# Ten more operands of layer 2 turned in squares, and the last stage's order made anew

## The chip, the core and the metric

The kernel runs on one core of a Trainium2 chip. Its time is the device time of one execution in microseconds (us). Five engines work at once, each through its own row of instructions, in order: TensorE (PE), VectorE (DVE), ScalarE (ACT), GpSimd (POOL) and SyncE (SP), which issues the DMAs. A semaphore makes one wait for another.

## What is computed

Two blocks stand in a layer, and there are two layers; the reference calls the layers' blocks A and B, twice over 2048 tokens of width 576, in single precision:

```python
x = A_x
x = x + _A_ref(_layernorm(x), A_wqkv, A_wo)                        # layer 1
x = x + _B_ref(_layernorm(x), B_w_q, B_k1, B_k2, B_u, B_v)
x = x + _A_ref(_layernorm(x), A_wqkv, A_wo)                        # layer 2
x = x + _B_ref(_layernorm(x), B_w_q, B_k1, B_k2, B_u, B_v)
```

A is linear attention with 32 heads of 18: q, k, v = x @ wqkv; phi(t) = (t + 1 if t > 0 else exp(t)) + 1e-6; kv = the sum over tokens of phi(k) v, z = the sum of phi(k); o = phi(q) kv / (phi(q) z + 1e-6); then o @ wo. B is a mixture of 64 experts, each one row of u and of v: for each of 32 heads the best of 8 first keys and of 8 second keys is picked (K = 1), and the output is the sum over the heads of gelu(x . u[e]) v[e]. The softmax over one pick is 1.

## The kernel before, in words

The 2048 tokens are 16 tiles of 128; the code numbers the layers 0 and 1, and a name such as `ppo1_7` is of layer 1 and tile 7. TensorE's products keep single precision by splitting each operand into two parts, hi and lo, and adding hi x hi, hi x lo and lo x hi (`product`, L258). An operand must have its channels on the partitions, so a tile of tokens is turned first. There are two ways:

- `transposed` (L215): TensorE turns five blocks of 128x128 into PSUM; ScalarE makes hi (L117), VectorE makes lo = source - hi (L118).
- `squares` over `moved`: VectorE turns the 20 squares of 32x32 of each 128x640 tile in place (L229, the tiles `rf`, `ro`, `rb`), SP stores the result (L231, `y_d`) and reads it back in four loads (L237) that put the squares where they belong, and the same two splits follow. The table `SQUARES` at the head of the kernel says which (layer, tile) take this way, for the operands f (input of k, v, q), o (input of the product with wo) and b (input of block B). `turned` chooses by it.

A tile's steps in block A of layer 2 are the late q (`lq`: product with the q weights, then phi on ScalarE, L284 to L286, and one sum on VectorE, L287), `num` (back_scale: GpSimd multiplies by z, L453, VectorE sums it, L456, inverts and multiplies, L460 and L461), `oT` (turning o), `O` (the product with wo, `ppo`, L483, then the residual x, L473, and the layer norm). In block B they are `bT` (turning y), `S` (scores, `pps`, L525), `sel` (VectorE picks the experts in 14 instructions, L553 to L590, whose last writes `cg`), `gel` (the gelu on ScalarE and GpSimd), the turning of `cg` by TensorE (in one transpose), and `po` (the product with v, L609, and the residual x, L473). In the kernel before, the token `bc1.2,0` turns the b of tile 2 and the cg of tile 0 in one group of six TensorE transposes and one pair of splits; `bT` and `cT` are the two apart, cT with one transpose (L512).

The order of the work is written out by hand: `play` runs the steps of a text in the order of its tokens (`x2` runs two pieces of a step at once), and `in_order` pins the order of PE, ACT, DVE and POOL to it. So no engine takes an instruction ahead of the one that stands before it. SP follows the order of the program. The last text holds the end of layer 0 and all of layer 1, from about 423 us on.

Of the kernel before, what the change touches and what calls it, by code (L numbers as in the profile page):

```python
# [64 lines left out]
def network(ctx, tc, x_in, wqkv, wo, wq_t, k_t, u_t, v2, c_mask, c_mask4, c_ident, c_code, c_code1, c_scale, c_shift, out):  # L65
# [809 lines left out]
    with in_order(*ALL):  # L875

        play("""
            bT0.13 gel0.12 po0.11 sel0.12 v1.10 po0.11x2 gel0.12 num0.15 sel0.12 k1.10 bT0.13 v1.10 sel0.12 fT1.11
            sel0.12 oT0.14 v1.10 fT1.11 O0.14 num0.15 cT0.12 num0.15 k1.10 cT0.12 O0.14 oT0.15 bT0.13 po0.12 S0.13
            O0.14 fT1.11 S0.13 oT0.15 po0.12x3 sel0.13x2 v1.11 gel0.13 fT1.12 gel0.13 oT0.15 O0.14 sel0.13x2 k1.11  # L880
            v1.11 O0.15 fT1.12 O0.15 bT0.14 st1.10 cT0.13 v1.11 bT0.14 S0.14 cT0.13 O0.15 fT1.12 keep1.12 po0.13 k1.11
            S0.14 gel0.14 sel0.14 po0.13 gel0.14 st1.11 po0.13 k1.12 sel0.14x2 po0.13 fT1.13 k1.12 O0.15 v1.12x2
            sel0.14 v1.12 bT0.15 cT0.14x2 st1.12 fT1.13 bT0.15 po0.14 S0.15 po0.14 fT1.13 S0.15 po0.14 ldx1.1 po0.14
            ldx1.3 v1.13 fT1.14 v1.13 sel0.15x3 gel0.15 k1.13 fT1.14 gel0.15 bT0.-1 v1.13 sel0.15 cT0.15 v1.14 cT0.15
            po0.15 k1.13 q1.13 bT0.-1 po0.15 q1.13 v1.14 po0.15x2 v1.14 k1.14 wl1.0 st1.13 fT1.15x2 k1.14 k1.15 v1.15
            rl1.0 st1.14 k1.15 ldq1.13 v1.15x2 rl1.2 st1.15 lq1.0 mk1.0 zs1.0 M1.1 rl1.1 lq1.0 M1.1 rl1.3 ldx1.0 zs1.0
            M1.4x2 M1.3 lq1.1 M1.0 num1.13 num1.0 num1.13 num1.0x2 M1.3 keep1.11 lq1.1 num1.1 M1.0 oT1.0x2 num1.1
            M1.2x2 rl1.4 num1.1 num1.13 lq1.2 O1.0 oT1.1 oT1.13 q1.14 lq1.2 O1.0 oT1.1 O1.0x2 num1.2 q1.14 lq1.3x2
            num1.2 oT1.13 bc1.0,-9 num1.3 O1.1 bc1.0,-9 num1.2 S1.0 O1.1 oT1.2 S1.0 num1.3 lq1.4 gel1.0 num1.3 oT1.2
            O1.1x2 O1.2 bc1.1,-9 sel1.0 gel1.0 ldx1.2 sel1.0 lq1.4 O1.13 rl1.6 bc1.1,-9 sel1.0 num1.4x2 S1.1 O1.2x2  # L890
            ldx1.13 O1.13 S1.1 lq1.6 O1.2 sel1.0 sel1.1 bc1.2,0 rl1.5 ldx1.5 rl1.7 num1.4 oT1.3 ldq1.14 lq1.5 lq1.6
            gel1.1 bc1.2,0 oT1.4 gel1.1 sel1.1 O1.13 rl1.8 sel1.1 S1.2 po1.0 oT1.3 lq1.5 sel1.1 S1.2 O1.3 po1.0 sel1.2
            rl1.9 O1.13 oT1.4 num1.6 bc1.13,1 num1.5 sel1.2 num1.5 lq1.7 bc1.13,1 gel1.2x2 num1.5 S1.13 O1.3 lq1.7
            O1.3x2 num1.6 rl1.11 sel1.2 po1.1 oT1.5 q1.15 oT1.5 ldx1.4 sel1.2 bc1.3,2 po1.1 S1.13 gel1.13 num1.6 O1.4
            bc1.3,2 sel1.13 q1.15 ldx1.6 po1.2 O1.5 oT1.6 ldq1.15 po1.2 sel1.13 num1.14 S1.3 O1.4 lq1.8 O1.4 num1.14
            num1.7 rl1.10 sel1.13 gel1.13 O1.5 num1.14 O1.4 num1.7 S1.3 sel1.13 ldx1.7 sel1.3 oT1.6 num1.7 bc1.4,13
            ldx1.14 bc1.4,13 rl1.12 O1.6 ldx1.8 lq1.8 po1.13 O1.5 gel1.3 O1.5 sel1.3 oT1.7 po1.13 sel1.3 num1.8 O1.6
# [59 lines left out]
```

## Time and profile before

| | us |
|---|---|
| median of three runs (lowest, highest) | 719.56 (718.05, 720.6) |
| the profiled execution | 718.14 |
| its span | 716.4 |
| TensorE busy in it | 699.6 |
| VectorE busy | 475.1 |
| ScalarE busy | 321.6 |
| GpSimd busy | 201.6 |

The span is the time from the first to the last instruction of the profile; 1.74 us lie around it. Busy time is the time in which an engine runs at least one instruction. In a row of the timeline, "x5" is a group of equal instructions run one after another, its length reaches from the first start to the last end, and "[0.48 <-DVE cg L590]" is idle time before it and what ended it. Tiles are named without their numbers in the profile, so `ptb<-ident,yb` is any tile's turning of b.

### The profile page before, as it was taken

How to read it: one execution, taken by the hardware profiler on the slowest of the kernel's cores; microseconds unless marked ns; L12 is line 12 of the kernel's file. 1: busy time of each engine (PE TensorE's matmuls, PEld its weight loads, DVE VectorE, ACT ScalarE, POOL GpSimd, SP SyncE). 2: the span in 40 equal slices, each digit the busy share in tenths (PEclk: the TensorE clock that was granted, in tenths of full speed). 3: DMA queues.
4: the chain of work that ended last, by engine and by line, in shares of the span. 5: the costliest groups of instructions: out<-in, count | busy, mean ns of one | idle time of the engine just before them, and what ended most of it. 6: DMA issues, size and time to landing. Idle time of an engine off the chain costs nothing.

```text
span 716.4 us, 14695 instructions
## 1 busy us (share of the span) xinstructions
PE 699.6 (98%) x5464; PEld 650.7 (91%) x5464; DVE 475.1 (66%) x1031; ACT 321.6 (45%) x658; POOL 201.6 (28%) x543
## 2 busy tenths in 40 slices
...
GB/s 270 291 164 243 266 234 262 247 192 175 108 1 64 103 101 91 162 216 215 245 218 233 212 196 175 168 44 128 149 120 84 97 86 125 47 67 34 67 17 66
DMA packets 82711, 107.17 MB, mean 150 GB/s; under 512 B 8976, under 2 KB 47376, under 8 KB 82640
## 3 DMA queue, kind: packets, MB, share of 16 engines
...
q14 instruction: 28, 0.23, 0.1%
...
## 4 chain that ended last, share of the span: by engine, by line
PE 82%; DVE 8%; ACT 4%; issue 2%; DMA 2%; POOL 1%; SPq 0%; DVEq 0%; ACTq 0%; POOLq 0%
PE ppk L258 15%; PE ppv L258 14%; PE ppq L258 14%; PE ppo L483 12%; PE pps L525 7%; PE kva L525 5%; PE kva L360 3%; PE fold_ps L641 2%; PE po L609 2%; PE ptb L215 2%; PE m L414 1%; PE pto L215 1%; DVE x L473 1%; PE ppq L270 1%; PE ppk L270 1%
## 5 line engine op out<-in xcount | busy, mean ns | idle before, releaser
L483 PE MATMUL ppo<-ohi,thio 126*128 126x252 f32 (+1 forms) x320 | 50.5, 300 | 2.6 <-ACT thio L117 2.6
L483 PEld LDWEIGHTS ppo<-ohi,thio 126*128 126x128 f32 (+1 forms) x320 | 44.8, 189 | 4.4 <-ACT thio L117 3.1
L258 PE MATMUL ppk<-whi,thif 128*128 128x252 f32 (+1 forms) x300 | 45.3, 298 | 0.8 <-ACT thif L117 0.8
L188 ACT ACTIVATE junk<-x,mb 128x576 bf16<-128x576 f32 x32 | 24.8, 775 | 45.2 <-POOL mb L187 44.9
L453 POOL TENSOR_TENSOR o<-pq,zb 128x576 f32<-128x576 f32 x19 | 27.4, 1441 | 62.2 <-ACT zb L399 58.6
L258 PE MATMUL ppv<-whi,thif 128*128 128x252 f32 (+1 forms) x300 | 44.7, 295 | 0.1
L258 PEld LDWEIGHTS ppk<-whi,thif 128*128 128x128 f32 x300 | 40.9, 188 | 4.0 <-issue 2.9
L205 ACT ACTIVATE yb<-x,rsb 128x640 f32<-128x640 f32 x32 | 29.5, 921 | 33.3 <-POOL rsb L195 33.3
L179 POOL TENSOR_SCALAR rsf<-mvf 128x1 f32<-128x1 f32 x16 | 3.4, 212 | 145.3 <-DVE mvf L176 145.2
L258 PE MATMUL ppv<-whi,tlof 128*128 128x252 f32 (+1 forms) x300 | 43.9, 293 | 0.0
L258 PE MATMUL ppk<-whi,tlof 128*128 128x252 f32 (+1 forms) x300 | 43.9, 293 | 0.0
L258 PEld LDWEIGHTS ppv<-whi,thif 128*128 128x128 f32 x300 | 41.3, 188 | 1.0 <-issue 0.4
L258 PEld LDWEIGHTS ppk<-whi,tlof 128*128 128x128 f32 x300 | 41.2, 188 | 0.0
L258 PEld LDWEIGHTS ppv<-whi,tlof 128*128 128x128 f32 x300 | 41.2, 188 | 0.0
L483 PE MATMUL ppo<-olo,thio 126*128 126x252 f32 (+1 forms) x256 | 39.6, 293 | 0.0
L258 PE MATMUL ppq<-whi 128*128 128x252 f32 (+1 forms) x260 | 39.5, 299 | 0.0
L483 PE MATMUL ppo<-ohi,tloo 126*128 126x252 f32 (+1 forms) x256 | 39.4, 293 | 0.0
L277 DVE TENSOR_SCALAR ek<-ek 128x576 f32<-128x576 f32 x16 | 7.3, 457 | 46.4 <-ACT ek L276 46.4
L258 PEld LDWEIGHTS ppq<-whi 128*128 128x128 f32 x260 | 36.0, 188 | 0.6 <-DVE eq L287 0.3
L483 PEld LDWEIGHTS ppo<-olo,thio 126*128 126x128 f32 x256 | 36.2, 188 | 0.0
L483 PEld LDWEIGHTS ppo<-ohi,tloo 126*128 126x128 f32 x256 | 36.1, 188 | 0.0
L258 PE MATMUL ppk<-wlo,thif 128*128 128x252 f32 x240 | 36.1, 293 | 0.0
(205 smaller groups left out, 1784.6 us busy)
## 6 DMA issues: line engine op xcount, KB each, us to landing
...
```

Source lines behind the costliest of these rows:

```text
L188: nc.scalar.activation(junk, xt, AF.Square, bias=m[:, 0:1], accum_out=m[:, 1:2])
L205: nc.scalar.activation(y, x2, AF.Identity, scale=rs[:, 0:1], bias=rs[:, 1:2])
L215: nc.tensor.transpose(pt[:, b * P:(b + 1) * P], x, ident)
L258: nc.tensor.matmul(o[:, at:at + c1 - c0], tt[a == "lo"][:, b, :], wb[:, cols + c0:cols + c1], start=(i == 0), stop=(i == len(todo) - 1))
L270: nc.tensor.matmul(p[:, at:at + c1 - c0], tt[a == "lo"][:, b, :], wb[:, cols + c0:cols + c1], start=(i == 0), stop=(i == len(todo) - 1))
L277: nc.vector.tensor_scalar(e, e, 1.0, EPS, op0=ALU.min, op1=ALU.add)
L360: nc.tensor.matmul(a[64 * h:64 * h + 64, c * 72:c * 72 + n], vt[:, 2 * c + h], fk[:, f0:f0 + n], start=(t == 0 and c == 0), stop=(t == NT ...
L453: nc.gpsimd.tensor_tensor(o[:, :D], pq, zb, op=ALU.mult)
L483: nc.tensor.matmul(p[:, at:at + c1 - c0], hl[a][:r, b], w[:r, c0:c1], start=(i == 0), stop=(i == len(todo) - 1))
L525: nc.tensor.matmul(p[:, :512], hl[a == "lo"][:, b, :], shi[:, b] if w == "hi" else slo[:, blocks(REM)[b][1]], start=(i == 0), stop=(i == l ...
L609: nc.tensor.matmul(p[:, at:at + c1 - c0], c[i], vmix[:, c0:c1], start=(i == 0 and not based), stop=(i == 1))
L641: nc.tensor.matmul(p[32 * j:32 * j + 32, at:at + c1 - c0], kpad[:, ch // 2, 24 - 8 * a:56 - 8 * a], st[:, c0:c1], start=(a == 0), stop=(a ...
```

## The change

Ten operands of layer 1 leave TensorE's way for the squares: o of tiles 3 to 6, and b of tiles 2 to 6 and 13. The six b stood in a group with a cg (bc), which is now turned alone. So TensorE loses 50 transposes, VectorE gains 10 transposes in squares and 6 small splits, ScalarE 6 small splits, and SP 10 stores and 40 loads.

```diff
 SQUARES = {
     "f": {(0, t) for t in range(4, NT)} | {(1, t) for t in range(3, 14)},
-    "o": {(0, t) for t in range(6, NT)},
-    "b": {(0, t) for t in range(5, 14)},
+    "o": {(0, t) for t in range(6, NT)} | {(1, t) for t in range(3, 7)},
+    "b": {(0, t) for t in range(5, 14)} | {(1, t) for t in range(2, 7)} | {(1, 13)},
 }
...
-            O1.1x2 O1.2 bc1.1,-9 sel1.0 gel1.0 ldx1.2 sel1.0 lq1.4 O1.13 rl1.6 bc1.1,-9 sel1.0 num1.4x2 S1.1 O1.2x2
+            cT1.0 oT1.3 oT1.4 lq1.6 sel1.1 po1.0 rl1.9 po1.0 gel1.1 oT1.4 lq1.5 lq1.6 gel1.1 bT1.2 O1.13 sel1.1 num1.5
...
```

The text of the last stage is new as a whole (40 lines); what it moves is seen on the engines. Names end in the number of a tile and a running number.

ScalarE around the split of the b of tile 2 (`thib1_2`) in layer 1, before; `eq1_5` and `eq1_6` belong to the phi of tiles 5 and 6:

```order
L284 ACTIVATE eq1_6_7428<-ppq1_6_7323 128x576
L285 ACTIVATE ppq1_6_7323<-ppq1_6_7323 128x576
L286 ACTIVATE eq1_6_7428<-eq1_6_7428 128x576
L539 ACTIVATE g1_1_7433<-s1_1_7309 128x64
L117 ACTIVATE thib1_2_7377<-ptb1_2_7370 128x768
L543 ACTIVATE g1_1_7433<-g1_1_7433 128x64
L188 ACTIVATE junk_85,mb1_13_7457<-x11_13_7319,mb1_13_7457 128x576
L117 ACTIVATE thio1_3_7395<-pto1_3_7389 128x640
L284 ACTIVATE eq1_5_7493<-ppq1_5_7399 128x576
L285 ACTIVATE ppq1_5_7399<-ppq1_5_7399 128x576
L286 ACTIVATE eq1_5_7493<-eq1_5_7493 128x576
L530 ACTIVATE s1_2_7483<-pps1_2_7468 128x512
```

And now:

```order
L286 ACTIVATE eq1_5_7486<-eq1_5_7486 128x576
L284 ACTIVATE eq1_6_7491<-ppq1_6_7429 128x576
L285 ACTIVATE ppq1_6_7429<-ppq1_6_7429 128x576
L286 ACTIVATE eq1_6_7491<-eq1_6_7491 128x576
L543 ACTIVATE g1_1_7475<-g1_1_7475 128x64
L117 ACTIVATE thib1_2_7347<-gb1_2_7342 128x640
L205 ACTIVATE yb1_13_7505<-x11_13_7335,rsb1_13_7501 128x640
L530 ACTIVATE s1_2_7531<-pps1_2_7516 128x512
```

The split of tile 2 stood after the phi of tile 6 and ahead of that of tile 5; now it comes behind the phi of tile 6 and the tanh of tile 1 (`g1_1`), and reads a loaded tile (`gb1_2`) in place of PSUM (`ptb1_2`).

TensorE at the same place, before: the end of a q product, then scores of tile 2 (`pps1_2`):

```order
L258 MATMUL ppq1_5_7399<-whi_76 128x324
L215 MATMUL pto1_4_7439<-ident_66,o1_4_7289 128x128 x5
L525 MATMUL pps1_2_7468<-shi_80,thib1_2_7377 128x512 x5
L525 MATMUL pps1_2_7468<-slo_81,thib1_2_7377 128x512 x4
L525 MATMUL pps1_2_7468<-shi_80,tlob1_2_7378 128x512 x5
L609 MATMUL po1_0_7485<-vmix_82,thib1_2_7377 128x252
L609 MATMUL po1_0_7485<-vmix_82,thib1_2_7377 128x324
L609 MATMUL po1_0_7485<-vmix_82,tlob1_2_7378 128x252
```

And now:

```order
L258 MATMUL ppq1_6_7429<-whi_76 128x324
L609 MATMUL po1_0_7464<-vmix_82,chi1_0_7404 128x252
L609 MATMUL po1_0_7464<-vmix_82,chi1_0_7404 128x324
L609 MATMUL po1_0_7464<-vmix_82,clo1_0_7405 128x252
L609 MATMUL po1_0_7464<-vmix_82,clo1_0_7405 128x324
L525 MATMUL pps1_2_7516<-shi_80,thib1_2_7347 128x512 x5
L525 MATMUL pps1_2_7516<-slo_81,thib1_2_7347 128x512 x4
L525 MATMUL pps1_2_7516<-shi_80,tlob1_2_7348 128x512 x5
L483 MATMUL ppo1_3_7534<-ohi_78,thio1_3_7411 128x252
```

The five transposes of o of tile 4 are gone from the row, `po1_0` has moved ahead of the scores, and the q product in front of them is that of tile 6 in place of tile 5.

VectorE near the split of the b of tile 4 (`tlob1_4`), before:

```order
L118 TENSOR_TENSOR tloo1_6_7825<-pto1_6_7818,thio1_6_7824 128x640
L460 RECIPROCAL r1_7_7943<-den1_7_7922 128x32
L461 TENSOR_TENSOR o1_7_7896<-eq1_7_7640,r1_7_7943 128x576
L118 TENSOR_TENSOR tlob1_4_7955<-ptb1_4_7947,thib1_4_7954 128x768
L287 SCALAR_TENSOR_TENSOR eq1_8_7993<-eq1_8_7993,ppq1_8_7861 128x576
L565 SCALAR_TENSOR_TENSOR m41_3_8016<-m1_3_7938 128x256
L567 SCALAR_TENSOR_TENSOR m21_3_8018<-m41_3_8016 128x128
L569 SCALAR_TENSOR_TENSOR cd1_3_8020<-m21_3_8018 128x32
L571 SCALAR_TENSOR_TENSOR m21_3_8018<-m21_3_8018 128x32
L473 SCALAR_TENSOR_TENSOR x21_13_8031,sumx21_13_8032<-po1_13_7998,x11_13_7319 128x576
L574 TENSOR_TENSOR oh1_3_8035<-cd1_3_8020,code_w_70 128x256
L577 TENSOR_TENSOR pr1_3_8037<-oh1_3_8035,m21_3_8018 128x512
```

And now:

```order
L571 SCALAR_TENSOR_TENSOR m21_3_8017<-m21_3_8017 128x32
L118 TENSOR_TENSOR tlob1_4_7972<-gb1_4_7966,thib1_4_7971 128x640
L229 STREAM_TRANSPOSE rb1_5_8032<-yb1_5_8030 128x5x4x32
L473 SCALAR_TENSOR_TENSOR x21_13_8043,sumx21_13_8044<-po1_13_8010,x11_13_7335 128x576
L287 SCALAR_TENSOR_TENSOR eq1_8_8047<-eq1_8_8047,ppq1_8_7906 128x576
L574 TENSOR_TENSOR oh1_3_8056<-cd1_3_8019,code_w_70 128x256
L577 TENSOR_TENSOR pr1_3_8058<-oh1_3_8056,m21_3_8017 128x512
L581 TENSOR_REDUCE pi1_3_8060<-pr1_3_8058 128x16
L473 SCALAR_TENSOR_TENSOR x11_6_8093,sumx11_6_8094<-ppo1_6_8064,x1_6_7896 128x576
L584 TENSOR_TENSOR ct1_3_8114<-pi1_3_8060,shift_71 128x64
```

A transpose in squares (`rb1_5`, the b of tile 5) now stands behind the split of tile 4, the select steps of tile 3 (`cd1_3`, `oh1_3`, `pr1_3`) are around it, and the residual of tile 13 (`x21_13`) comes ahead of the phi sum of tile 8.

TensorE in the layer before, near the scores of tile 14 (`kva1`, written with `thib0_14`; other rows of `kva1` are the state of layer 1), before:

```order
L483 MATMUL ppo0_15_6073<-olo_79,tloo0_15_5954 128x324
L215 MATMUL ptb0_14_6112<-ident_66,yb0_14_6029 128x128 x5
L360 MATMUL kva1_3751<-ek1_10_5905,v5_0_86 64x72 x8
L360 MATMUL kva1_3751<-ek1_10_5905,v5_0_86 64x36 x2
L512 MATMUL ptc0_13_6130<-ident_66,cg0_13_6040 128x128
L525 MATMUL kva1_3751<-shi_80,thib0_14_6118 128x512 x5
```

And now:

```order
L483 MATMUL ppo0_15_6073<-olo_79,tloo0_15_6004 128x324
L215 MATMUL ptb0_14_6105<-ident_66,yb0_14_6064 128x128 x5
L512 MATMUL ptc0_13_6123<-ident_66,cg0_13_6069 128x128
L525 MATMUL kva1_3751<-shi_80,thib0_14_6111 128x512 x5
L525 MATMUL kva1_3751<-slo_81,thib0_14_6111 128x512 x4
L525 MATMUL kva1_3751<-shi_80,tlob0_14_6112 128x512 x5
```

The state products of tile 10 (`ek1_10`) have left their place between the transposes and the scores.

## Rows read from the trace of the kernel before

**Rows 1.** The page, part 1: busy time, share of the span, number of instructions.
```profile
PE 699.6 (98%) x5464; PEld 650.7 (91%) x5464; DVE 475.1 (66%) x1031; ACT 321.6 (45%) x658; POOL 201.6 (28%) x543
```

**Rows 2.** Busy time of each engine (matmuls in brackets), granted clock, DMA, 550 to 700 us.
```profile
550.00:700.00 150.00, 148.91 (x993) 138.22 (x992) 132.32 (x314) 68.94 (x133) 59.09 (x166) 1.00 0.21 68
```

**Rows 3.** Timeline of TensorE, 599 to 614 us: start, length, line, output<-inputs.
```profile
599.89 1.56 PE L483 MATMUL ppo<-ohi,thio 126*128 126x252 f32 x10
...
603.63 0.42 PE L609 MATMUL po<-vmix,thib 128*128 128x252 f32 x2
...
604.15 0.71 PE L215 MATMUL pto<-ident,o 128*128 128x128 f32 x5
604.62 1.41 PE L525 MATMUL pps<-shi,thib 128*128 128x512 f32 x5
...
607.98 0.71 PE L215 MATMUL pto<-ident,o 128*128 128x128 f32 x5
608.53 0.71 PE L215 MATMUL ptb<-ident,yb 128*128 128x128 f32 x5
609.71 0.33 PE L215 MATMUL ptb<-ident,cg 128*128 128x128 f32 x1 [0.48 <-DVE cg L590]
609.81 1.57 PE L258 MATMUL ppq<-whi 128*128 128x252 f32 x10
...
613.59 1.33 PE L525 MATMUL pps<-shi,thib 128*128 128x512 f32 x5
```

**Rows 4.** By source line, L229, L118, L117: count, shortest/median/longest ns, first and last start.
```profile
L229 DVE STREAM_TRANSPOSE rb<-yb x9: 835/845/846, 295.5 to 423.1; 128x640 f32<-128x640 f32 x9
...
L118 DVE TENSOR_TENSOR tlob<-ptb,thib x25: 284/944/958, 234.9 to 711.2; 128x768 fp32r<-128x768 f32 x14, 128x640 fp32r<-128x640 f32 x9, 128x128 fp32r<-128x128 f32 x2
...
L118 DVE TENSOR_TENSOR clo<-ptc,chi x16: 251/292/294, 252.9 to 478.7; 128x128 fp32r<-128x128 f32 x16
...
L118 DVE TENSOR_TENSOR tlob<-gb,thib x9: 782/818/822, 306.1 to 436.6; 128x640 fp32r<-128x640 f32 x9
...
L117 ACT ACTIVATE thib<-gb x9: 727/738/742, 303.7 to 434.6; 128x640 fp32r<-128x640 f32 x9
```

**Rows 5.** Timeline of ScalarE, the phi of a late q at 668 us.
```profile
667.81 0.65 ACT L284 ACTIVATE eq<-ppq 128x576 f32<-128x576 f32 x1 [1.35 <-PE ppq L258]
...
668.93 0.67 ACT L286 ACTIVATE eq<-eq 128x576 f32<-128x576 f32 x1
```

**Rows 6.** Timeline of VectorE, 598 to 617 us; 41 instructions from first to last.
```profile
598.56 0.42 DVE L553 TENSOR_TENSOR mt<-s 128x256 f32<-128x256 f32 x1 [1.53 <-ACT s L530]
...
602.87 0.74 DVE L287 SCALAR_TENSOR_TENSOR eq<-eq,ppq 128x576 f32<-128x576 f32 x1
...
604.58 0.74 DVE L473 SCALAR_TENSOR_TENSOR x<-po,x 128x576 f32<-128x576 f32 x1
...
617.04 0.34 DVE L590 TENSOR_TENSOR cg<-g,ct 128x128 f32<-128x128 f32 x1
```

**Rows 7.** Timeline of one square (tile 13, operand f): its transpose, its split.
```profile
461.85 0.84 DVE L229 STREAM_TRANSPOSE rf<-yf 128x640 f32<-128x640 f32 x1 [1.23 <-DMA wob<-in_wo]
...
468.96 0.74 ACT L117 ACTIVATE thif<-gf 128x640 fp32r<-128x640 f32 x1 [2.57 <-DMA gf<-y_df]
```

**Rows 8.** Timeline of VectorE and GpSimd, 562 to 574 us.
```profile
562.53 0.19 DVE L569 SCALAR_TENSOR_TENSOR cd<-m 128x32 bf16<-128x32 bf16 x1
...
571.16 2.82 POOL L453 TENSOR_TENSOR o<-eq,zb 128x576 f32<-128x576 f32 x2
571.29 1.34 DVE L569 SCALAR_TENSOR_TENSOR cd<-m 128x32 bf16<-128x32 bf16 x1
...
572.56 1.48 DVE L571 SCALAR_TENSOR_TENSOR m<-m 128x32 bf16<-128x32 bf16 x1
```

**Rows 9.** Timeline of TensorE, two waits of the layer before.
```profile
456.04 0.81 PE L360 MATMUL kva<-ek,v 128*64 128x72 f32 x20 [0.44 <-ACT g L539]
...
492.08 1.58 PE L258 MATMUL ppk<-whi,thif 128*128 128x252 f32 x10 [0.79 <-ACT thif L117]
```

More of the change, by code (lines that the diff above doesn't have):

```diff
@@ L883, in network @@
[L883 to L887, printed above, removed]
@@ L908, in network @@
[L908 to L911 removed]
+            bT0.13 po0.11 gel0.12 sel0.12 v1.10 po0.11 sel0.12 k1.10 gel0.12 po0.11 sel0.12 fT1.11 sel0.12 bT0.13
@@ new lines, in network @@
+            num0.15 v1.10 oT0.14 v1.10 O0.14 num0.15 cT0.12 num0.15 k1.10 cT0.12 oT0.15 O0.14 fT1.11 bT0.13 po0.12x2
+            S0.13 fT1.11 S0.13 sel0.13x3 v1.11 oT0.15 O0.14 po0.12x2 k1.11 gel0.13 fT1.12 gel0.13 oT0.15 O0.14 sel0.13
+            v1.11 O0.15x2 bT0.14 fT1.12 v1.11 bT0.14 cT0.13 fT1.12 cT0.13 S0.14 keep1.12 k1.11 S0.14 gel0.14x2
+            po0.13x3 sel0.14 O0.15 k1.12 st1.11 st1.10 sel0.14x3 po0.13 fT1.13x2 k1.12 O0.15 v1.12x2 cT0.14 v1.12
+            st1.12 cT0.14 bT0.15x2 po0.14 S0.15 po0.14x2 fT1.13 S0.15 po0.14 v1.13 fT1.14 v1.13 sel0.15x2 gel0.15x2
```

55 lines of the change are left out of this document (27 added, 28 removed).

## The prediction

> **What bounds the kernel now.** I read the busy table first. TensorE is busy for 699.6 of 716.4 us, VectorE for 475.1 [rows 1]: over the whole run TensorE sets the time, and the 50 transposes that go would be worth their whole length. But the change acts between about 550 and 650 us, so the second view is the busy time of that stretch: from 550 to 700 us TensorE is busy for 148.9 and VectorE for 132.3 of 150 us, at a granted clock of 1.00 [rows 2]. VectorE has 17.7 us to spare there, 12%, and the change takes from the engine with nothing to spare and gives to the one with little. Third, the order of time on TensorE in that stretch [rows 3]: matmuls follow one another with no gap except at 609.71, where the last of six transposes waits 0.48 us for VectorE's cg. So VectorE is already the late one at places. Last come the durations by source line [rows 4], and the neighbours on ScalarE and VectorE [rows 5, 6].
>
> The sum below is made against the profiled execution's own 718.14 us (a span of 716.4 and 1.74 around it). The median of the runs shown is 719.56, 1.42 higher, and I add that at the end. A measurement of this kernel can tell about 0.3% from no change, 2.2 us.
>
> **What goes from TensorE.** Ten operands lose five transposes of 128x128 each, 50 in all. Five of them take 0.55 us from start to start (607.98 to 608.53 [rows 3]), so ten groups are 10 x 0.55 = 5.5 us. The six cg transposes that hung on six of these groups stay, now alone. Everything on TensorE in this stretch is on the path, so this is -5.5 us until something else is late.
>
> **What comes to VectorE and ScalarE.** Each operand gets a transpose in squares of 0.84 us. The six split of b and cg together (0.95, `tlob<-ptb`, 944 ns at the median) become one of b (0.82) and one of cg (0.29) [rows 4]. VectorE gets 10 x 0.84 + 6 x (0.82 + 0.29 - 0.94) = 8.4 + 1.0 = 9.4 us. ScalarE splits the same operands and six small ones more; it is busy for 321.6 of 716.4 us [rows 1], so its sums are hidden, but the order of its row matters (below). SP issues ten stores and 40 loads more, between loads of x, pq and of kept operands. A store waits in SP's row for its transpose in squares and a load for its store, and what stands behind them waits too; but the order has those other loads well ahead of their readers, so I cost it at nothing, from 0 to 0.5 us.
>
> 132.3 + 9.4 = 141.7 us of VectorE work would stand in 150 - 5.5 = 144.5 us: 98% busy. Two engines, each at 98%, can't both keep that while each waits for the other, so the order decides where they meet. I went through it at the two places where cover looks thin.
>
> **First place: the scores of tile 2.** In the kernel before, ScalarE splits tile 2's b (`thib1_2`) before the phi of tile 5, with a whole product on TensorE in between. Now the split stands behind the three phi operations on `ppq1_6` and a tanh, and on TensorE only the four matmuls of `po1_0` lie between the end of `ppq1_6` and `pps1_2`. A phi chain takes from 667.81 to 669.60 [rows 5], 1.79; the tanh (about 0.2) and the split of a loaded square (0.738 [rows 4]) follow: 2.7 us. The cover is po, 603.63 to 604.15, 0.52 [rows 3]. TensorE waits 2.7 - 0.5 = 2.2 us. Bounds: 1.5, if the tanh is done before phi ends and the operations overlap by the 0.1 us that their reported times do, and 3.0, if ScalarE is also a little late to phi. I take 2.2, the plain difference.
>
> **Second place: from `po1_2` to `ptc1_4`.** VectorE's residual of tile 2 needs `po1_2`; from it to cg of tile 4, which `ptc1_4` needs, its row holds 45 instructions in a fixed order. Forty of them stand in the row of before as well, between 598.56 and 617.38: 41 instructions there, with no wait among them, 18.8 us [rows 6]. The difference: `tloo1_14` goes (-0.82 [rows 4], the value of a 640 wide split); the residual of tile 2 (+0.74), the phi sum of tile 9 (+0.74), both as long as the rows shown [rows 6], the split of cg 3 (+0.29), and two transposes in squares (+1.68) come; two splits of b are 0.13 shorter each (-0.26). That makes 18.8 + 2.4 = 21.2 us; the added durations overlap a little with the next start, and I take 20.9.
>
> TensorE's work in between, from rows 3: po 0.52, the output product 3.74 (599.89 to 603.63), scores 3.36 (604.62 to 607.98), two groups of transposes 1.10, one cg 0.11, a q product 3.78 (609.81 to 613.59), scores 3.36, po 0.52, all 16.5 us. TensorE waits 20.9 - 16.5 = 4.4 us, whether at `ptc1_3`, `pps1_5` or `ptc1_4`. In the kernel before the same stretch cost 0.48 (609.71), which goes. Bounds: 3.0, if the row is passed with the shortest times of each operation, and 7, if VectorE comes to the residual already a pair of operations behind and meets GpSimd once (below). I take 4.4 - 0.5 = 3.9.
>
> **The other squares.** From the start of a transpose in squares to the start of ScalarE's split, a square took 461.85 to 468.96, 7.1 us, of which TensorE's own way has about 1.3 [rows 7]. Between the output product and the scores of tile 3 TensorE has 19 us of other work, and the others are similar. I count 0 to 1 us for all of them, and take 0.5, the nearer to what I can see for tile 3.
>
> **The layer before.** Two waits of the rows before it change: 0.44 at 456.04 and 0.79 at 492.08 [rows 9]. The state products (0.81 long [rows 9]) are moved away from the one and put in front of the other, and one set is taken from between the transposes and the scores of tile 14, which then wait for ScalarE about as long as that set was. -0.44 - 0.79 + 0.8 = -0.4; bounds -1.2 and +0.5.
>
> **Sum.** -5.5 + 2.2 + 3.9 + 0.5 - 0.4 = +0.7. 718.14 + 0.7 = 718.8 in a profile, 720.3 as a median. The ends of all terms: -5.5 + 1.5 + 2.5 + 0 - 1.2 = -2.7, and -5.5 + 3.0 + 6.5 + 1.0 + 0.5 + 0.5 (SP) = +6.0.
>
> **Contention, on which the slower side rests.** At 571.16 GpSimd runs two 128x576 products (L453) for 2.82 us, and two 128x32 operations of VectorE in that time take 1.34 and 1.48 us; the first took 0.19 at 562.53 [rows 8]. VectorE lost about 2.4 us to one pair. While VectorE has spare time this costs little; in a stretch that VectorE sets, each such us is one of the kernel's. The splits of a square read the loaded tile and the hi part, both in SBUF, where those of a TensorE transpose read PSUM. In the rows by line none of the nine `tlob<-gb` is long (782 to 822 ns [rows 4]), but they ran before 437 us, mostly without those products beside them.
>
> The Trainium skill, SBUF — State Buffer (Who interferes with whom), has a rule that speaks against the change: a VectorE instruction with two SBUF inputs contends with a GpSimd instruction that reads SBUF, and the second to start is blocked until the first is done. The small operations at 571.29 and 572.56 agree with it. By that rule ten splits more enter the class; if two or three of them met a product and lost 1.2 us each, the sum would be +3 to +4 and not +0.7.
>
> **Rivals.**
> - *The cover holds.* ScalarE and VectorE reach both places early enough, and only the removed transposes count: -5.5 - 0.4 = -5.9, 712.2 in a profile, 713.7 as a median. For it: VectorE has 2.8 us left by the sums. Against it: both waits follow from rows that stand in order with no free choice. 0.12.
> - *Half of it holds.* One of the two places costs what I say and the other half or less: -2.5, about 717. 0.20.
> - *Forecast:* the waits give back what the transposes saved: 718 to 722, likeliest 720.3. 0.45.
> - *VectorE is blocked by GpSimd where it sets the time.* One mechanism: L453's products meet the splits and select steps between `po1_2` and `ptc1_4`. The price is up to 2.4 us for each pair (rows 8); from one pair on, it decides: 720.3 + 2.4 = 722.7, with two 725. For it: the product of tile 8 stands in GpSimd's row inside the stretch, those of tiles 14 and 7 just ahead of it and that of tile 15 at its end. Against it: in the same 18.8 us of before (rows 6) no operation was long. 0.23.
>
> No change lies between 719.56 - 2.16 = 717.4 and 721.7. Faster: 0.12 and two thirds of 0.20 make 0.25; slower: nearly all of 0.23 and a fifth of the forecast make 0.32; the rest, 0.43, is the same. The range goes from 715.0 to 724.0: it leaves out most of the first rival, and of the last the cases with two pairs or more.
>
> **What would show it.** In the changed kernel's profile: 5 transposes fewer for each of ten operands; a wait of some 2 us of `pps` for ScalarE's `thib` at the scores of tile 2; waits of `ptc` for cg, or of the next products, of 4 us in all where tile 3 and 4 of layer 1 are selected, VectorE being busy above 95% in that stretch; and long VectorE rows where L453 runs. The forecast is wrong if those waits are under 1 us each (then the kernel is faster by most of 5.5), or if VectorE shows idle time in the stretch while TensorE waits: then transfers, not VectorE, were late.

## The result, and the profile after

The changed kernel takes 722.05 us (median of six executions, 721.04 to 723.49) against 719.39 us for the kernel before (six executions, 718.05 to 720.6). The ratio is 1.0038, with a 95% interval of [1.0027, 1.0050]: it is slower, by 2.7 us. The profiled execution took 721.04 us with a span of 719.3, so 2.9 us more than that of before.

The busy line of the page of the changed kernel, which answers to [rows 1]:

```profile
PE 696.6 (97%) x5414; PEld 646.3 (90%) x5414; DVE 479.2 (67%) x1047; ACT 323.7 (45%) x664; POOL 206.0 (29%) x543
```

The 50 transposes are gone from TensorE, and its busy time fell by 3.0 us, yet the span grew by 2.9. So TensorE is idle for some 6 us more. The profiled execution of the changed kernel is the fastest of its six. To see where, I cut both profiles at the same instructions: the first product with wo of tile 14 in layer 0, the first score of tile 1 in layer 1, and the last score group. The first stretch runs up to the score of tile 1, the second from there to the last score group. First the kernel before; the columns are stretch and length, busy time of TensorE, its weight loads, VectorE, ScalarE and GpSimd (with instructions), granted clock, DMA share and GB/s:

```profile
430.39:551.02 120.63, 118.52 (x920) 111.98 (x919) 68.64 (x139) 57.78 (x114) 28.43 (x77) 1.00 0.41 124
551.02:700.78 149.76, 147.89 (x986) 137.20 (x985) 132.12 (x313) 69.72 (x134) 59.09 (x166) 1.00 0.22 70
```

The changed kernel, cut at the same instructions:

```profile
430.70:550.53 119.83, 118.16 (x920) 111.96 (x919) 69.00 (x141) 58.13 (x115) 29.52 (x77) 1.00 0.46 134
550.53:703.59 153.06, 146.40 (x940) 133.85 (x939) 136.61 (x325) 71.38 (x140) 62.16 (x165) 0.99 0.34 103
```

Both stretches together went from 270.39 to 272.89 us, +2.50; the other 0.4 us of the profiles lie before and behind. TensorE's idle time rose from 2.11 + 1.87 = 3.98 to 1.67 + 6.66 = 8.33, by 4.35; its busy time fell by 1.85 and not by 5.5. (Of the 3.0 us of the page, 1.1 fell behind the last scores, where one product less stands; it has moved into the second stretch.) The granted clock of the second stretch, 0.99, is the first hint at why. Two places carry most of it, and both are those of the prediction.

**The first place**, the scores of tile 2, on TensorE of the changed kernel (rows as in [rows 3]):

```profile
561.57 0.43 PE L609 MATMUL po<-vmix,clo 128*128 128x252 f32 x2
564.11 1.44 PE L525 MATMUL pps<-shi,thib 128*128 128x512 f32 x5 [2.11 <-ACT thib L117]
565.38 1.85 PE L525 MATMUL pps<-slo,thib 128*128 128x512 f32 x4
567.03 2.16 PE L525 MATMUL pps<-shi,tlob 128*128 128x512 f32 x5
569.03 1.49 PE L483 MATMUL ppo<-ohi,thio 126*128 126x252 f32 x10
```

The wait is 2.11 us, and ScalarE's row shows why, as in [rows 5]: the phi of tile 6 and the tanh stand ahead of the split.

```profile
561.50 0.65 ACT L284 ACTIVATE eq<-ppq 128x576 f32<-128x576 f32 x1 [0.97 <-PE ppq L258]
...
563.19 0.24 ACT L543 ACTIVATE g<-g 128x64 f32<-128x64 f32 x1
563.33 0.72 ACT L117 ACTIVATE thib<-gb 128x640 fp32r<-128x640 f32 x1
```

But the scores then take 4.92 us (564.11 to 569.03), where those of before took 3.36 (604.62 to 607.98, [rows 3]). The last number but two of a row of the windows, us by us, is the granted clock:

```profile
565.00:566.00 1.00, 1.00 (x5) 0.82 (x4) 0.54 (x3) 0.09 (x1) 0.87 (x3) 0.72 0.61 212
566.00:567.00 1.00, 1.00 (x3) 0.74 (x3) 0.14 (x1) 0.83 (x1) 1.00 (x1) 0.50 0.71 173
...
569.00:570.00 1.00, 1.00 (x9) 0.97 (x8) 0.07 (x1) 0.77 (x2) 0.00 (x0) 1.00 0.42 159
```

From 565.4 to 568.9 TensorE has the lower of its two levels, 1.2 GHz (0.50). A wait of 2.11 us was followed by 1.56 us more of slow matmuls, which count as busy time. Nothing on TensorE's row says so: the rows are only longer. This is one execution; the mean granted clock of the six goes from 0.992 to 0.997, and the profiled one has 0.993, so not every execution need have the fall.

**The second place**, from `po1_2` to `ptc1_4`; the waits on TensorE, of which the fourth stands just behind it:

```profile
600.36 1.59 PE L483 MATMUL ppo<-ohi,thio 126*128 126x252 f32 x10 [0.40 <-ACT thio L117]
...
610.46 0.30 PE L512 MATMUL ptc<-ident,cg 128*128 128x128 f32 x1 [1.80 <-DVE cg L590]
...
620.30 0.30 PE L512 MATMUL ptc<-ident,cg 128*128 128x128 f32 x1 [1.79 <-DVE cg L590]
...
625.35 0.53 PE L609 MATMUL po<-vmix,clo 128*128 128x252 f32 x2 [0.21 <-DVE clo L118]
```

They make 4.2 us (4.0 without the fourth), where the stretch of before had 0.48 [rows 3]. VectorE's row of that stretch, from the residual of tile 2 to the cg of tile 4, has no wait in it, as in [rows 6]: it is busy for 19.97 of 20.86 us, 96%. The third row stands behind it:

```profile
599.30 0.76 DVE L473 SCALAR_TENSOR_TENSOR x<-po,x 128x576 f32<-128x576 f32 x1
...
619.87 0.29 DVE L590 TENSOR_TENSOR cg<-g,ct 128x128 f32<-128x128 f32 x1
...
622.37 1.33 DVE L556 TENSOR_TENSOR mx<-mt 128x64 f32<-128x64 f32 x1
```

599.30 to 620.16 is 20.86 us, against 20.9 forecast. The third row is one that GpSimd holds up, as in [rows 8]: 1.33 us, where the same operation takes 0.23 at 602.59, while GpSimd runs this:

```profile
622.15 1.48 POOL L453 TENSOR_TENSOR o<-pq,zb 128x576 f32<-128x576 f32 x1
```

It comes two us too late to count in the second place.

### The profile page after: what moved, and what is told of

It is laid out like the page before. It is cut to its first block, busy times and chain, and to the rows that moved or that the text cites. A ratio compares the mean times of both kernels' runs of the same rounds, so it can differ in the third digit from the quotient of the medians.

```text
span 719.3 us, 14709 instructions
## 1 busy us (share of the span) xinstructions
PE 696.6 (97%) x5414; PEld 646.3 (90%) x5414; DVE 479.2 (67%) x1047; ACT 323.7 (45%) x664; POOL 206.0 (29%) x543
## 4 chain that ended last, share of the span: by engine, by line
PE 84%; DVE 6%; ACT 4%; DMA 2%; issue 2%; POOL 1%; SPq 1%; DVEq 0%; ACTq 0%; POOLq 0%
PE ppq L258 15%; PE ppo L483 14%; PE ppk L258 13%; PE ppv L258 13%; PE pps L525 9%; PE kva L525 5%; PE kva L360 3%; PE fold_ps L641 2%; PE po L609 2%; PE ptb L215 2%; PE m L414 1%; DMA go<-y_do 1%; PE ppq L270 1%; PE ppk L270 1%; PE pto L215 1%
## 5 line engine op out<-in xcount | busy, mean ns | idle before, releaser
L453 POOL TENSOR_TENSOR o<-pq,zb 128x576 f32<-128x576 f32 x19 | 27.4, 1442 | 64.9 <-ACT zb L399 61.2
L258 PE MATMUL ppv<-wlo,thif 128*128 128x252 f32 x240 | 36.1, 293 | 0.0
```

Source lines behind the costliest of these rows:

```text
L258: nc.tensor.matmul(o[:, at:at + c1 - c0], tt[a == "lo"][:, b, :], wb[:, cols + c0:cols + c1], start=(i == 0), stop=(i == len(todo) - 1))
L453: nc.gpsimd.tensor_tensor(o[:, :D], pq, zb, op=ALU.mult)
```

## The experiments

Each ratio is to the kernel before, timed in the same session. "The stretch" is the time from the first product with wo of tile 14 to the last scores, as above, in the one profile of each kernel: before 270.39, after 272.89. It repeats well where nothing is changed: from the transpose of the cg of tile 4 to the scores at 688.39 the changed kernel takes 68.09 us, and e1, e2, e3 and e5 take 68.06 to 68.15. The times spread more: the intervals of e1, e2, e3, e4, e6 and e8 overlap with the [1.0027, 1.0050] of the changed kernel, so what is said of a gain in them rests on the profiles. Of an order line, only the tokens around the edit are printed.

**e1: the split of tile 2 ahead of the phi of tile 6.**

```diff
-oT1.4 lq1.5 lq1.6 gel1.1 bT1.2 O1.13
+oT1.4 lq1.5 bT1.2 lq1.6 gel1.1 O1.13
```

> The changed kernel, with one edit: the split of the b of tile 2 stands ahead of the phi of tile 6 on ScalarE (and its lo part ahead of that phi's sum on VectorE). My theory: the scores of tile 2 waited 2.11 us only for this split's place, and the wait also made the granted clock fall to 0.50 for some 3 us, in which the scores took 4.92 us in place of 3.36. Both go: 722.05 - 2.1 - 1.6 = 718.4, scores start at once after po, clock 1.00 throughout 560 to 570. Rival 1 (the clock fell for another reason, such as the DMA traffic of 184 GB/s there): only the wait goes, 720.0, and 0.50 stays somewhere in that stretch. Rival 2 (the time saved is waited for later, since VectorE sets 598 to 620): 721 to 722, with longer waits of ptc for cg.

1.0024 [1.0007, 1.0042]; stretch 272.06. The wait of 2.11 and the slow clock are both gone, 3.7 us, but the stretch is only 0.8 shorter. Two waits on TensorE are new:

```profile
574.86 1.43 PE L525 MATMUL pps<-shi,thib 128*128 128x512 f32 x5 [0.50 <-ACT thib L117]
...
587.48 0.80 PE L483 MATMUL ppo<-ohi,thio 126*128 126x252 f32 x4 [1.62 <-DVE clo L118]
```

The second comes out of VectorE's row, where the split of a square is twice as long as its usual 0.82 and the small split, whose end frees a PSUM tile, stands behind it:

```profile
585.48 1.74 DVE L118 TENSOR_TENSOR tloo<-go,thio 128x640 fp32r<-128x640 f32 x1 [0.62 <-ACT thio L117]
587.14 0.28 DVE L118 TENSOR_TENSOR clo<-ptc,chi 128x128 fp32r<-128x128 f32 x1
```

On GpSimd at that time:

```profile
585.12 1.42 POOL L453 TENSOR_TENSOR o<-pq,zb 128x576 f32<-128x576 f32 x1
```

So TensorE gets to VectorE's next late result earlier, and waits there. The kernel takes 720.66 us, not the 718.4 of my theory. As the second rival has it, the time saved is waited for later, but for `clo` and not for cg: those waits stay at 1.79.

**e2: eight products into an unused half of the same PSUM tile, in the wait.** They compute nothing that is used.

```diff
+        if (l, t) == (1, 2):
+            for _ in range(8):
+                nc.tensor.matmul(p[:, 512:], shi[:, 0, :P], shi[:, 0], start=True, stop=True)
```

> The changed kernel, with eight matmuls of no use (128x512, some 0.22 us each) put into the wait ahead of the scores of tile 2, written to the unused half of their PSUM tile. The split's place is as in the changed kernel. If idle time of TensorE is what lets the clock fall, the clock stays at 1.00, the scores take 3.4 us and the kernel is 1.5 us faster (720.5), though the wait for the split stays (now mostly filled). If something else sets the clock there, nothing changes (722.0), or it is slower by what the eight overrun.

1.0024 [1.0011, 1.0037]; stretch 272.58. TensorE of this kernel:

```profile
562.78 2.00 PE L526 MATMUL pps<-shi 128*128 128x512 f32 x8
565.05 1.43 PE L528 MATMUL pps<-shi,thib 128*128 128x512 f32 x5 [0.27 <-ACT thib L117]
```

With the wait filled the clock stays at 1.00 and the scores take 3.39 us (565.05 to 568.44), so the fall costs 1.5 us at that place. That the filling kept the clock up isn't shown by this one profile: in e8, below, the same wait of 2.11 us stays empty, and no fall follows either. The stretch won only 0.3: 1.02 us came back as a wait at 588.35, for the same `clo` as in e1, and again behind a split that is twice as long, beside a product L453 of GpSimd that runs from 585.99 to 587.42:

```profile
586.41 1.69 DVE L118 TENSOR_TENSOR tloo<-go,thio 128x640 fp32r<-128x640 f32 x1 [0.68 <-ACT thio L117]
```

**e3: the six transposes in squares of b left out.** The store takes y as it is, so the b of these tiles is not turned.

```diff
+LEFT_OUT = {f"b1_{t}" for t in (2, 3, 4, 5, 6, 13)}
...
-        nc.vector.transpose(r.rearrange("p (j b c) -> p b j c", j=4, b=NB), at)
+        if n not in LEFT_OUT:
+            nc.vector.transpose(r.rearrange("p (j b c) -> p b j c", j=4, b=NB), at)
+        else:
+            r = y
```

> The changed kernel without the six transposes in squares of VectorE for b of layer 1 (SP stores the tile as it is; so this part of the turning is left out and the loads bring unturned squares). VectorE has 5.0 us less to do, 1.68 of it between po1_2 and ptc1_4. If VectorE's row sets that stretch, its waits (0.40 + 1.80 + 1.79 + 0.21) shrink by 1.7 to 2.5 in sum and the kernel takes 719.5 to 720.3. If it is a matter of the loads or of ScalarE, the waits stay and the time is within 0.5 us of 722.05.

1.0031 [1.0019, 1.0043]; stretch 273.29: no gain at all, and the waits for cg stay at 1.80 and 1.66. VectorE from the residual of tile 2 to the cg of tile 4:

```profile
602.18 0.76 DVE L479 SCALAR_TENSOR_TENSOR x<-po,x 128x576 f32<-128x576 f32 x1
...
609.14 0.76 DVE L293 SCALAR_TENSOR_TENSOR eq<-eq,ppq 128x576 f32<-128x576 f32 x1 [0.18 <-ACT eq L292]
...
611.87 0.73 DVE L590 TENSOR_TENSOR ct<-pi,shift 128x64 int32<-128x64 int32 x1
...
620.20 0.36 DVE L466 RECIPROCAL r<-den 128x32 f32<-128x32 f32 x1 [0.34 <-POOL den L463]
...
622.65 0.29 DVE L596 TENSOR_TENSOR cg<-g,ct 128x128 f32<-128x128 f32 x1
```

The stretch of VectorE is 20.76 us, with 1.7 us of work less in it. VectorE waits for ScalarE and for GpSimd, and one small operation runs 0.73 instead of 0.22 us beside GpSimd's L453. So "VectorE's operations take 20.9 us" was too simple: the same row, with 1.7 us of work less, hits other limits 0.1 us below.

**e4: e1, and the last select steps of tiles 3 and 4 moved ahead in VectorE's row.**

```diff
-num1.8 gel1.4 lq1.9 bT1.6 num1.8 lq1.9 sel1.4 oT1.14
+num1.8 gel1.4 lq1.9 sel1.4 num1.8 bT1.6 lq1.9 oT1.14
-sel1.3 num1.8 O1.6x2 S1.4x2 sel1.3 oT1.14
+sel1.3 num1.8 O1.6 S1.4x2 sel1.3 O1.6 oT1.14
```

> The edit of the first run (split of tile 2 ahead of the phi of tile 6), and VectorE's row in the second stretch in another order with the same instructions: the last select steps of tile 3 ahead of the residual of tile 6, those of tile 4 ahead of 1/den, o of tile 8, the transpose of tile 6 and the phi sum of tile 9. By my theory the row, not its length alone, sets the two waits of ptc for cg: the first falls from 1.80 by 0.7, the second from 1.79 to about 0.1, after which pto1_8 waits 0.6 for o; with the first edit 718.4 - 0.7 - 1.1 = 716.6, faster than both kernels. Rival: VectorE has the same work, so what is put behind cg is waited for later: 718.0 to 718.5.

1.0053 [1.0033, 1.0074], no better than the changed kernel's 1.0038; stretch 274.82, 1.9 longer. TensorE at the cg of tile 3, and the clock behind it:

```profile
610.63 0.39 PE L512 MATMUL ptc<-ident,cg 128*128 128x128 f32 x1 [2.38 <-DVE x L473]
```

```profile
612.00:613.00 1.00, 1.00 (x7) 1.00 (x6) 0.96 (x2) 0.00 (x0) 0.85 (x3) 0.50 0.65 249
```

The transpose no longer waits for cg but for the residual x of tile 6, which now stands behind cg and frees the PSUM tile that the transpose writes. What is moved ahead in a full row puts something else behind. The time is 723.4 us, where 716.6 was expected.

**e5: e1, and cT of tile 2 ahead of oT of tile 5,** so that the small split no longer stands behind the blocked one.

```diff
-num1.14 oT1.5 cT1.2x2 oT1.6
+num1.14 cT1.2x2 oT1.5 oT1.6
```

> The edit of e1 (split of tile 2 ahead of the phi of tile 6) and one more: the split of cg 2 (chi, clo) ahead of that of o of tile 5. In e1 a part of the gain came back as a wait of 1.62 us of the output product of tile 5, which ended with clo of cg 2: that clo stood on VectorE behind the lo split of o of tile 5, which waited 0.62 for its square's loads and then took 1.74 (0.82 is usual) while GpSimd ran L453. Theory: clo frees the PSUM tile that the product of tile 5 takes; with clo ahead the wait is 0 to 0.4, VectorE comes to po1_2 some 1 us earlier, and the kernel takes 719.4 (e1 720.7 less 1.3). Rival: the square's arrival itself holds the product, and the wait stays at 1.0 or more: 720.3 to 720.7.

1.0010 [0.9997, 1.0023]; stretch 272.82. The wait of 1.62 is gone, and up to the scores of tile 3 the kernel is 2.4 us ahead of the changed one (38.44 us from the first scores of tile 1, for 40.88). Then the next wait is this:

```profile
597.02 0.30 PE L512 MATMUL ptc<-ident,cg 128*128 128x128 f32 x1 [1.14 <-DVE cg L590]
```

```profile
600.00:601.00 1.00, 1.00 (x6) 1.00 (x6) 0.97 (x3) 0.74 (x1) 0.83 (x2) 0.50 0.90 288
```

The clock fell at 599 to 603, and the cg waits of 1.24 and 1.79 follow. By the ratio it is the best of the orders with ten squares, and the only one of them whose interval lies below that of the changed kernel; but the interval overlaps with that of e1, and the stretch is only 0.1 shorter than the changed kernel's. 719.4 us were expected, 720.71 measured.

**e6: e5, and the residual of tile 13 added by TensorE** (a product with the unit matrix, placed in the wait for cg, and ScalarE copies out), so VectorE has one 128x576 operation less.

```diff
-po1.2x2 num1.7 oT1.6 sel1.3 po1.13 sel1.3 bT1.4
+po1.2x2 num1.7 oT1.6 sel1.3x2 bT1.4
...
-oT1.7x2 gel1.4
+oT1.7x2 base1.13 po1.13 gel1.4
...
```

> The edits of e5, and the residual of tile 13 taken from VectorE: TensorE adds x to the product (two matmuls against the unit matrix, 1.1 us) in the wait ahead of the transpose of cg 3, and ScalarE copies the sum out; the product of tile 13 stands there too. VectorE has 0.75 us less between po1_2 and cg 3, TensorE 1.1 more in its 1.8 us wait. If VectorE's row sets the stretch, ptc for cg 3 and for cg 4 come 0.65 to 0.75 earlier: 718.7 (e5's 719.4 less 0.7). If, as in e3, what VectorE is spared is waited for elsewhere (GpSimd's den, ScalarE's phi, a PSUM tile), no gain against e5, or 0.4 slower.

1.0034 [1.0018, 1.0050]; stretch 272.48. No gain: TensorE waits 0.88, 1.08 (now for ScalarE's split of an o) and 1.25 us, and the clock fell at 600 to 604.

**e8: GpSimd's L453 of five tiles replaced by a copy on ScalarE.** The multiplication by z of these tiles is left out.

```diff
-        nc.gpsimd.tensor_tensor(o[:, :D], pq, zb, op=ALU.mult)
+        if l == 1 and t in (7, 8, 9, 14, 15):
+            nc.scalar.activation(o[:, :D], pq, AF.Copy)
+        else:
+            nc.gpsimd.tensor_tensor(o[:, :D], pq, zb, op=ALU.mult)
```

> The changed kernel with the GpSimd product L453 of tiles 7, 8, 9, 14 and 15 of layer 1 replaced by a copy on ScalarE (the multiplication by z is left out). GpSimd has 5 x 1.43 us less. If VectorE is held up by GpSimd in the stretch that it sets (the slower rival of the prediction), the long rows there (0.91 at 587.95, 1.33 at 622.37, 1.15 at 627.36) fall to their usual 0.46, 0.23 and 0.42, and the kernel is 1 to 2 us faster: 720 to 721. If those rows fall but TensorE's waits at 600 to 625 stay, contention isn't what holds it: 721.5 to 722.3.

1.0016 [1.0004, 1.0028]; stretch 270.85, 2.0 shorter than that of the changed kernel. But it isn't the collisions that went from the second place. VectorE there:

```profile
598.36 0.76 DVE L476 SCALAR_TENSOR_TENSOR x<-po,x 128x576 f32<-128x576 f32 x1
...
618.90 0.29 DVE L593 TENSOR_TENSOR cg<-g,ct 128x128 f32<-128x128 f32 x1
```

20.83 us, where it was 20.86. TensorE of the same stretch:

```profile
564.70 1.44 PE L528 MATMUL pps<-shi,thib 128*128 128x512 f32 x5 [2.11 <-ACT thib L117]
...
609.50 0.30 PE L515 MATMUL ptc<-ident,cg 128*128 128x128 f32 x1 [1.78 <-DVE cg L593]
609.72 1.68 PE L258 MATMUL ppq<-whi 128*128 128x252 f32 x10
...
615.04 1.33 PE L528 MATMUL pps<-shi,thib 128*128 128x512 f32 x5
...
619.34 0.30 PE L515 MATMUL ptc<-ident,cg 128*128 128x128 f32 x1 [0.34 <-DVE cg L593]
```

And the granted clock at the two waits:

```profile
564.00:568.00 4.00, 3.30 (x14) 2.71 (x15) 2.68 (x7) 1.57 (x3) 3.56 (x7) 1.00 0.87 262
611.00:615.00 4.00, 4.00 (x21) 4.00 (x20) 3.79 (x10) 2.64 (x6) 1.77 (x5) 0.57 0.13 48
```

The wait at the scores of tile 2 is 2.11 again, but here no clock fall follows: 1.5 us saved. The fall came after the wait for the cg of tile 3: the q product takes 5.32 us (609.72 to 615.04) and not 3.87 (610.59 to 614.46 in the changed kernel). The wait for the cg of tile 4 is shorter by the same 1.45, 0.34 and not 1.79. So a slow TensorE inside the second place cost nothing here: the place kept the length of VectorE's row, 20.8 us.

The run shows two things more. The gain of 1.5 us at the first place stayed, while in e2, with the same scores of 3.39 us, most of it came back. Between the scores of tiles 2 and 3, e8 takes 25.78 us and e2 27.08. The product L453 that ran beside the split of the o of tile 5 in e2 is one of the five, and the split has its usual length again, with no wait of TensorE behind it:

```profile
585.29 0.82 DVE L118 TENSOR_TENSOR tloo<-go,thio 128x640 fp32r<-128x640 f32 x1
```

And behind the second place, from the transpose of the cg of tile 4 to the scores with the wait of 0.35, e8 takes 67.53 us in place of 68.09: the two long rows of VectorE at 622.37 and 627.36 (1.33 and 1.15) take 0.23 and 0.41 there, and the wait of 0.21 is gone. So GpSimd's products do cost the changed kernel some 0.5 us, behind the second place, and by these rows they took back most of what e2 had won. The copies on ScalarE are new work, so this is the balance of both.

**e9: e5, and the lo split of the b of tiles 4 to 6 on GpSimd.**

```diff
-        split(g.rearrange(...), ...)
+        split(g.rearrange(...), ...,
+              nc.gpsimd if n in ("b1_4", "b1_5", "b1_6") else nc.vector)
```

> The edits of e5, and the lo split of the squares of b of tiles 4, 5 and 6 done by GpSimd in place of VectorE. VectorE has 3 x 0.74 = 2.2 us less in 590 to 626, two of the three in the stretch that it sets. If the length of VectorE's row is all: 1.5 us faster than e5, 717.9. If GpSimd (2.0 us for one such split, by the one at 11.4 us) blocks VectorE's operations with two SBUF inputs meanwhile, some of them last over 1 us more, and it is as slow as e5 or slower: 719.5 to 721.

1.0078 [1.0063, 1.0093]; stretch 275.47, the slowest. GpSimd, then VectorE:

```profile
602.12 1.56 POOL L118 TENSOR_TENSOR tlob<-gb,thib 128x640 fp32r<-128x640 f32 x1
```

```profile
602.20 1.57 DVE L557 TENSOR_TENSOR mx<-mt 128x64 f32<-128x64 f32 x1
```

The split takes 1.56 us there, and holds a 0.23 us operation of VectorE for 1.57: at this one VectorE gave away 0.82 and lost 1.34. Of the other two, the one at 629.65 holds an operation of 0.42 for 1.32, and the one at 616.75 holds none. The waits for cg grew to 3.31 and 1.91.

**e10: the order of before, with only o of tiles 3 to 6 in squares.**

```diff
-    "o": {(0, t) for t in range(6, NT)},
+    "o": {(0, t) for t in range(6, NT)} | {(1, t) for t in range(3, 7)},
...
```

The diff is to the kernel before; the rest of it moves only the `oT` of these tiles. The squares land in an unused part of `wlo`, here and in the next three.

> The order of the kernel before, with the four operands o of tiles 3 to 6 of layer 1 alone turned in squares (their b stay on TensorE with cg, and the landing place of the four is a part of the q, k, v weights' tile that layer 1 no longer uses). Each square's transpose stands right behind its o, its split where the split of TensorE's transposes stood, so TensorE has 20 transposes less (2.2 us) and VectorE 3.4 us more between 540 and 600, where it has about 3.7 of 30 us free from 569 to 599 and more ahead of it. If what spoils the whole change is the order's two places (split of tile 2, the stretch from 598 to 621) and not the squares as such: 2 us faster than before, 717.3. If VectorE gives back what it gets also here: within 0.7 of before, 718.7 to 719.8, with waits for thio or clo at the products of tiles 3 to 6.

1.0054 [1.0034, 1.0074]; stretch 275.22. This one was misplaced by me. Its square of tile 5 on VectorE, ScalarE and VectorE:

```profile
580.59 0.85 DVE L229 STREAM_TRANSPOSE ro<-o 128x640 f32<-128x640 f32 x1 [0.71 <-POOL o L467]
```

```profile
588.56 0.74 ACT L117 ACTIVATE thio<-wlo 128x640 fp32r<-128x640 f32 x1 [2.84 <-DMA wlo<-y_do]
```

```profile
589.33 0.82 DVE L118 TENSOR_TENSOR tloo<-wlo,thio 128x640 fp32r<-128x640 f32 x1 [4.52 <-ACT thio L117]
```

The way through memory took 8.0 us, and the split stood too early in VectorE's row: VectorE, and behind it TensorE (4.40 for a cg), waited for DMA. It can't say whether four squares in a better place pay, but shows what a square costs whose split isn't late enough: with the clock fall behind the wait, the stretch is 4.8 us longer than before.

**e11, e12, e13: the order of before, and few o in squares:** tiles 3 and 4 (e11), 13 as well (e12), 6 as well (e13). The diff is that of e11 to the kernel before.

```diff
-    "o": {(0, t) for t in range(6, NT)},
+    "o": {(0, t) for t in range(6, NT)} | {(1, t) for t in range(3, 5)},
...
-num1.3 oT1.2 O1.1x2
+num1.3 oT1.3x2 oT1.2 O1.1x2
-num1.4 oT1.3 ldq1.14
+num1.4 oT1.4x2 ldq1.14
-bc1.2,0 oT1.4 gel1.1
+bc1.2,0 gel1.1
```

> As the run with o of tiles 3 to 6, but only tiles 3 and 4 (10 transposes, 1.1 us, and 1.7 us more on VectorE, between 540 and 575, where it is busy for some 18 of 30 us). If squares are free while VectorE has room: 718.4, 1.1 faster than before. If not: 719.2 to 719.8.

> The run with o of tiles 3 and 4 alone, and the o of tile 13 turned in squares too; its transpose stands at 525 us or so, where VectorE is busy for 17 of 30 us, and 11 us of TensorE's work lie between it and its split. TensorE has 15 transposes less than before (1.65 us). If squares are free where VectorE has room and the split stands 8 us or more behind the transpose: 0.5 faster than with tiles 3 and 4 alone, 1.6 faster than before (ratio 0.9977). Rival: the time saved is waited for at the select steps of 600 to 621, where the wait for cg had grown from 0.48 to 0.94 with tiles 3 and 4: no faster than with these alone (ratio 0.9983 or more).

> As the run with o of tiles 3, 4 and 13, and o of tile 6 in squares as well, whose transpose (0.84) falls near 590 us, where VectorE is busy for 9 tenths and more. If VectorE's room decides, the 0.55 us that TensorE is spared come back as a longer wait for cg near 610: no faster than with 3, 4 and 13, up to 0.8 slower. If only the distance from transpose to split matters (10 us here): 0.5 faster, ratio 0.9970.

e11: 718.88 us, 0.9983 [0.9971, 0.9994], stretch 270.01. e12: 718.65, 0.9998 [0.9985, 1.0011], stretch 269.73. e13: 719.31, 0.9995 [0.9983, 1.0008], stretch 269.97. The one wait in the second place of e11:

```profile
611.25 0.33 PE L215 MATMUL ptb<-ident,cg 128*128 128x128 f32 x1 [0.94 <-DVE cg L594]
```

It was 0.48 before [rows 3]: half of what the ten transposes gave is already lost in it. The three intervals overlap, and none goes more than 0.3% under the kernel before; only e11's ends below 1, and the stretch, 0.4 to 0.7 shorter in all three, points the same way. Beyond two squares nothing more is won that could be measured. e11's ratio is that of the 1.1 us expected; the 1.6 us of e12 and the ratio of 0.9970 of e13 didn't come.

## Why the prediction was right and wrong

The forecast was 718.8 in a profile and 720.3 as a median; 721.04 and 722.05 were measured. By its own limits (no change up to 721.7) that is slower, to which it gave 0.32, and not the same, to which it gave 0.43. Both waits came where they were forecast, and for the engine named. Step by step, on the stretch's +2.50; the time of a row on TensorE is counted from its start to the next start, without idle time:

| term | forecast | measured |
|---|---|---|
| transposes off TensorE (of o, b and cg) | -5.5 | -5.1 |
| first place, the wait | +2.2 | +2.1 |
| first place, the clock behind it | 0 | +1.6 |
| second place, with the 0.21 behind it | +3.9 | +3.7 (4.2 - 0.48) |
| the other squares, waits of TensorE | +0.5 | 0 |
| layer before, idle time | -0.4 | -0.4 (2.11 to 1.67) |
| a unit-matrix product ahead of the last scores | 0 | +1.1 |
| the last waits, behind 681 us | 0 | -1.0 (1.39 to 0.35) |
| TensorE's other rows | 0 | +0.6 |

The measured column adds up to +2.6, 0.1 off by rounding.

- **The step that failed is the price of the first place, "TensorE waits 2.7 - 0.5 = 2.2 us".** The wait was 2.11, but the place cost 3.7, because TensorE ran at 0.50 for most of the 3.5 us after it. Its upper bound, 3.0, was passed too. I had read the granted clock of 1.00 in [rows 2] as given, though it was that of a TensorE idle for 1.09 of 150 us. Nor is the fall certain: e8 has the same wait and no fall.
- **TensorE's busy time fell by less than 5.5.** It fell by 1.85; without the 1.56 of the slow scores that is 3.4. The transposes themselves saved 5.1, 0.51 for each operand: [rows 3] have one group at 0.55 (607.98 to 608.53) and one at 0.47 (604.15 to 604.62), and I had priced all at 0.55. The new order moves a unit-matrix product of 1.12 us into the stretch. And rows of `po` that stand at a wait are 1.0 us longer in all: two `po` take from 598.48 to 599.96 in the changed kernel, 1.48 us, while one takes 0.52 in [rows 3]. The other rows are 0.4 shorter.
- **The second place was right in place and size,** and e8 shows its mechanism best: with TensorE slowed by 1.45 us inside it, its length stayed. e3 limits it: the 20.9 us aren't only VectorE's own work, since 1.7 us less of that brought 0.1.
- **The other squares:** ScalarE waited 7.6 us for their loads between 550 and 640 us, but no wait of TensorE came of it, so 0 is right for the 0.5.
- **The layer before** came out at -0.4 by luck. Of the two waits named, the 0.79 is gone but for 0.05, and the 0.44 is still 0.36. A wait of 0.81 at 435.16, which I hadn't costed, fell to 0.37, and four new ones of 0.15 to 0.31 came.
- **The last waits** got shorter because the new order moves that unit-matrix product, which had stood behind the last scores, into a wait of 0.96 us ahead of them. I hadn't costed it; in the stretch it costs 0.1, and behind it nothing is won. Before, then after:

```profile
700.78 1.44 PE L525 MATMUL pps<-shi,thib 128*128 128x512 f32 x5 [0.96 <-ACT thib L117]
```

```profile
702.47 1.14 PE L598 MATMUL po<-x,ident 128*128 128x252 f32 x4
```

- **The rival of GpSimd's contention** doesn't hold as it was put: in the changed kernel no VectorE operation between 599.30 and 619.87 is long, and e8 leaves that stretch at 20.83. The mechanism exists: in e1 it turned a split of a square from 0.82 into 1.74 us. By the Trainium skill, SBUF — State Buffer (Who interferes with whom), a VectorE instruction with two SBUF inputs and a GpSimd instruction that reads SBUF contend, and the second to start waits for the first; e1's rows agree, the split ending at 587.22 after a product that ends at 586.54. In the changed kernel it cost some 0.5 us behind the second place, and in e1 and e2 it took back part of what the first place had given (e8).

Which of the terms is the cause? Taken away one by one, each gives little: the first place 0.8 of its 3.7 us (e1), the clock fall 0.3 of 1.5 (e2), six of the transposes in squares nothing (e3), a further order nothing beyond e1 in the stretch (e5). Only with five of GpSimd's products gone as well did the 1.5 us of the clock stay (e8). The terms of the sum aren't separate: TensorE that comes earlier waits at the next late result. So much is shown: where the change gives back what it saves, and that no single one of these takes the loss away.

The runs with fewer squares don't lose (e11 to e13), but they differ from the changed kernel in more than the number: they keep the order of before, turn only o, and land the squares elsewhere. And e10, with four squares, has a longer stretch than the changed kernel with ten (275.22 and 272.89), so their places count as well as the number. That the loss comes from the sum of the work which the change puts between TensorE's products (9.4 us on a VectorE that was already at 88% in that stretch, and the way through memory) is therefore argued and not shown, and e3 speaks against VectorE's part alone: 5.0 of the 9.4 us less gained nothing. Whether an order exists in which all ten squares pay stays open.
